# A transformer block in float32 on one core: part of the first MLP product by seven products of quarters in place of eight

## The chip, the core and the metric

The kernel runs on one core of a Trainium2 chip. The core has a matrix engine (TensorE, with its weight loads), VectorE, ScalarE, GpSimd (POOL in the profile) and SyncE (SP), which here issues nearly all transfers. [...] The metric is the device time of one execution in microseconds.

## The reference

One block: a layer norm without weights, attention, a second layer norm and an MLP, each with a residual. There are 2048 rows of 512, and 32 heads of 16.

```python
h = x + A(layernorm(x))
h2 = h + B(layernorm(h))

# A: qkv = x @ wqkv; each position attends to 8 positions at distances 0, 2, .. 14 behind it
logits = einsum("bhsd,bhswd->bhsw", q, kg) * Dh**-0.5      # masked where idx < 0
o = einsum("bhsw,bhswd->bhsd", softmax(logits), vg)
return o @ wo

# B: 512 -> 1792 -> 512, squared relu
h = x @ w1 + b1
r = where(h > 0, h, 0)
return (r * r) @ w2 + b2
```

## The kernel before

**Precision.** A float32 product is made of three passes in TensorE's faster float32 form: each operand is split into a high part (a cast by ScalarE) and the low rest (a subtraction by GpSimd or VectorE), and high x high, low x high and high x low are added in PSUM. `mm3` issues the three passes, each over four blocks of 128 in the contraction (`KB`).

**Tiles and stages.** The rows stand in 16 tiles of 128, in four groups `u` of four tiles (512 rows). First come qkv for all tiles. The attention of a group (`item`) is VectorE's and GpSimd's work and runs well ahead of its group's MLP. `to_mlp(u)` turns the attention's result, multiplies it with `wo` (`wo_product`), normalises, and turns the rows to the form the MLP wants; `split_h` then writes the high and low parts into the first four of twelve blocks of `big_h` and `big_l`.

**The MLP of a group.** The 1792 features are 14 blocks `f` of 128. For each, `mlp1(f)` multiplies w1's block with the group's 512 rows: 12 matmuls with 512 moving columns into one bank. ScalarE applies bias and relu, squares and casts, and the low part follows. `mlp2(f)` multiplies the result with w2's block: 12 matmuls into four banks (`acc`, one for each row tile), two blocks behind `mlp1` (`LAGW`). w1 is split once and stays: six blocks in `w1a_h`/`w1a_l`, eight in the other blocks of `big_h`/`big_l`. w2 is split once, written to DRAM, and read again for each block and group (`get_w2`, buffers `pair`). In the loop over `f` of group `u`, after block `TO_MLP`, stands `to_mlp(u + 1)`.

**The order.** Nothing of the order is written out by hand. Every operation is a task of `Plan`, with a duration for each engine that can do it, what it reads and writes, and the buffers that it takes (`bufs` has their numbers: six PSUM banks `ps`, one `qp`; the logits and exponentials `le` hold the eighth bank all the time). `deadlines` goes backwards from the TensorE tasks, whose places in time are the running sum `plan.pe`, and gives each task a due time with a random part (`NOISE`, one `SEED`). `schedule` is a list scheduler in simulated time: at each step the engine that can start first takes the ready task with the earliest due time. A transfer may start only `AHEAD` us before it is due; `KEEP` row buffers of a class are held back for more urgent tasks; `BEFORE` says how far ahead of its group the attention is due; `W2_EACH` spaces w2's splits; `X_BY_DRAM` lists the row tiles that are turned for qkv by DRAM and VectorE in place of TensorE. The instructions are then emitted in order of their simulated starts, and each engine and SP's queue run theirs strictly in that order. Semaphores come from the framework by what is read and written.

**What the profile's lines are.** L457 is the matmul in `mm`, of `mm3` (qkv, `wo`, first MLP product); L735 the matmul in `mlp2`; L955 the two half products at the very end; L401 a transpose by TensorE; L322 a cast (`hi`), L327 a low part (`lo`), L332 any sum through `tt`; L722, L724 relu and square; L572, L577, L603, L621 the attention.

Of the kernel before, what the change touches and what calls it, by code (L numbers as in the profile page):

```python
# [9 lines left out]
F32 = mybir.dt.float32  # L10
# [38 lines left out]
SEM = 0.15  # L49
AHEAD = 7.0  # L50
WAIT = {"DVE": 1.2, "ACT": 0.6, "POOL": 1.6, "SP": 0.8}
KEEP = 5
BUSY = 1.1
# [24 lines left out]
class Plan:  # L78
# [50 lines left out]
    def deadlines(self):  # L129

        draw = random.Random(SEED)
        for t in reversed(self.tasks):
            d = min([s.alap for s in t.succs], default=1e6) - t.dur - t.lat - WAIT.get(t.only, 1.0)
            t.alap = t.pe if t.pe is not None else d if t.by is None else min(d, t.by)
            t.due = t.alap + draw.uniform(-NOISE, NOISE)

    def schedule(self):
# [6 lines left out]
        for t in self.tasks:  # L144
            for b in t.bufs:
# [4 lines left out]
        queue = {tag: sorted((t for t in self.tasks if any(b.tag == tag for b in t.new)),  # L150
                             key=lambda t: t.due) for tag in (*ROWS, "pair")}
        while ready:
# [29 lines left out]
            if not best:  # L182
                held = {}
                for t in order:
                    for b in t.bufs:
                        if users[b]:
                            held.setdefault(b.tag, {})[b] = t
                raise RuntimeError([(o.n, round(o.start), round(o.due)) for o in order
                                    if o.on == "PE"][::40], [(t.n, [b.tag for b in t.new]) for t in ready][:12],
                                   {k: [(t.n, users[b]) for b, t in v.items()]  # L190
                                    for k, v in held.items()})
# [53 lines left out]
def block_kernel(ctx, tc, x, wqkv, wo, w1, b1, w2, b2, out):  # L245
# [23 lines left out]
    def where(t):  # L269
# [19 lines left out]
    w1a = (w1a_h, w1a_l)  # L289
    le = psum.tile([P, 2, R * W * GH], F32, name="le")  # L290

    bufs = {**ROWS, "pair": 4, "unit": 1, "kv": 3, "q": 1, "pr": 3, "o": 2, "ps": 6, "qp": 1,
            "st": 2, "mv": 4, "rs": 4, "sv": 6, "mx": 2, "sm": 2}
    pools = dict.fromkeys(("st", "mv", "rs", "sv", "mx", "sm"), small)
    pools.update(ps=psum, qp=psum, unit=wpool, pair=wpool)
    plan = Plan(bufs)
# [11 lines left out]
    def act(n, fn, extra=0.0, **k):  # L308
        return plan.add({"ACT": ac(n) + extra}, lambda e: fn(), **k)
# [232 lines left out]


    def window(t, i0, *ap):
        return bass.AP(tensor=t.tensor, offset=t.offset + i0 * GC,
                       ap=[list(t.ap[0]), [GC, IQ], [GC, W], *ap])

    def item(u, g, due, o):
# [17 lines left out]
        win(2, vs)  # L566
        lg = lambda: le[:, 0].rearrange("p (i w h) -> p i w h", i=R, w=W)
        ex = lambda: le[:, 1].rearrange("p (i w h) -> p i w h", i=R, w=W)
        lgs = [("lg", 0), ("lg", IQ)]
        for n, i0 in enumerate((0, IQ)):  # L570
            pr = buf("pr", (P, IQ, W, GC), name="pr")
            vec(2048, lambda pr=pr, i0=i0: nc.vector.tensor_tensor(  # L572
                out=pr.get(),
                in0=qp.get()[:, i0:i0 + IQ].unsqueeze(2).to_broadcast([P, IQ, W, GC]),
                in1=window(ks.get(), i0, [1, GC]), op=ALU.mult),
                r=[qp, ks], w=[pr], by=due + 5 * n)
            vec(2048, lambda pr=pr, i0=i0: nc.vector.tensor_reduce(  # L577
                out=lg()[:, i0:i0 + IQ].rearrange("p i w h -> p (i w h)"),
                in_=pr.get().rearrange("p i w (h d) -> p (i w h) d", d=DH), axis=X, op=ALU.add),
                r=[pr], w=[("lg", i0)], by=due + 5 * n + 1)  # L580
        if u < 2:
# [7 lines left out]
           ALU.subtract, r=[mx], w=lgs, by=due + 6)  # L589
        act(256, lambda: nc.scalar.activation(le[:, 1], le[:, 0], AF.Exp, scale=DH ** -0.5),  # L590
            r=lgs, w=["ex"], by=due + 6)
        vec(300, lambda: nc.vector.tensor_reduce(
            out=sm.get(), in_=ex().rearrange("p i w h -> p i h w"), axis=X, op=ALU.add),
            r=["ex"], w=[sm], by=due + 8)
        vec(64, lambda: nc.vector.reciprocal(sm.get(), sm.get()), w=[sm], by=due + 8)
        tt("DVE", 256, ex, ex, lambda: sm.get().unsqueeze(2).to_broadcast([P, R, W, GH]),
           ALU.mult, r=[sm], w=["ex"], by=due + 8)
        own = o is None
        if own:
            o = buf("o", (P, R, GC), name="o")  # L600
        for i0 in (0, IQ):
# [3 lines left out]
                in0=ex()[:, i0:i0 + IQ].unsqueeze(4).to_broadcast([P, IQ, W, GH, DH])),  # L605
                r=["ex", vs], w=[p2], by=due + 9 + i0)
            w = W // 2
# [50 lines left out]

    to_split = []

# [4 lines left out]
    def wo_product(t, oh, ol, h, pe, **k):  # L665
        ps = buf("ps", (P, D), name="wo")
        mm3(ps, ps.get, D, oh, ol, (lambda k: wo_h[:, k, :], [("wo", 0, k) for k in range(KB)]),
# [14 lines left out]
        def parts():  # L682
            if pe:
                view, src = lambda p: hh(p)[:, :, i, :], ht.get
            else:
# [3 lines left out]
               w=keys[1], engs=("DVE",) if pe else ("POOL", "DVE"))  # L689
        to_split.append(parts)  # L690


# [35 lines left out]

    def mlp2(f, hid, w2s, acc, js, first, last, split_):
        rh, rl = hid  # L730

        def run(terms, r, lead, end):
            def go(e):
                for n, (l, wn, j) in enumerate(terms):
                    nc.tensor.matmul(acc[j].get(), l.get()[:, j * P:(j + 1) * P],  # L735
                                     w2s.get()[:, wn], start=lead and n < len(js),
                                     stop=end and n >= len(terms) - len(js))
            plan.add({"PE": len(terms) * 0.23}, go, r=r, w=[acc[j] for j in js])
# [170 lines left out]
    split_h()  # L909
    w2s = {}  # L910
    for u in range(NU):
# [4 lines left out]
        engs = ("POOL", "DVE") if last else LO  # L916
        for f in range(FB):
            if u == 0 and f + FA < FB:
                w1_job(FA + f)
            w2s[f] = get_w2(f)  # L920
            hid[f] = mlp1(f, ("DVE",) if last and f >= FB - LAGW else engs)
            if f >= 2:
                g = f - 2
                if last and g == FB - 1 - LAGW:
                    mlp2(g, hid[g], w2s[g], acc, range(R - 1), g == 0, False, True)
                    mlp2(g, hid[g], w2s[g], acc, [R - 1], g == 0, True, False)
                else:
                    mlp2(g, hid[g], w2s[g], acc, range(R), g == 0, False, True)
            if not last and f == TO_MLP:
                to_mlp(u + 1, need[u + 1])  # L930
# [66 lines left out]
```

## Time and profile before

| | us |
|---|---|
| median of 3 runs | 515.17 (514.84 to 515.93) |
| the profiled execution | 514.67 |
| its span from first to last instruction | 512.9 |
| TensorE busy in it | 501.9 (98%) |
| VectorE, ScalarE, GpSimd busy | 333.6, 292.0, 323.0 |
| TensorE's clock, share of full | 1.00 |

The span is what the trace covers; 1.8 us of the profiled execution lie outside it. A matmul's busy time is its whole latency, and matmuls overlap, so the interval from start to start is what one costs in a row of them. A row of a group gives the line, engine, operation, tiles and shapes, the count, the busy time, the mean of one in ns, then the engine's idle time before them and what ended it.

### The profile page before, as it was taken

The numbers are of one execution on the slowest core, as the hardware profiler recorded it, in microseconds if no ns is written. First come the engines' busy times: TensorE is split into PE (matmuls) and PEld (weight loads), VectorE is DVE, ScalarE is ACT, GpSimd is POOL, SyncE is SP. The second block draws the span as 40 slices with busy tenths as digits, with TensorE's granted clock in tenths as the row PEclk, the third lists the DMA queues.
The fourth block names the chain that finished last, engine by engine and source line by source line (L and its number), as shares of the span: only waits on it lengthen the run. The fifth ranks groups of instructions, "written<-read, shape, count | busy, mean of one in ns | idle before, by whom it ended". The sixth has DMA issues, their size and how long they took to land.

```text
span 512.9 us, 6775 instructions
## 1 busy us (share of the span) xinstructions
PE 501.9 (98%) x2300; PEld 419.2 (82%) x2300; DVE 333.6 (65%) x314; ACT 292.0 (57%) x552; POOL 323.0 (63%) x273
## 2 busy tenths in 40 slices
PE   8999999999998999999999999999999999999997
PEld 8998888888886888868888877888888887888885
DVE  6259898996979996988799979596022103446003
ACT  4538877759364654379843436974367645433341
POOL 6421659768697799899994789589755424223220
PEclk9999999999999999999999999999999999999999
DMA  7699698999979999768976486865462731999422
GB/s 243 179 277 297 148 301 274 348 356 402 335 290 334 326 363 353 224 224 300 324 258 220 168 289 237 272 217 184 129 203 86 251 116 41 305 358 408 160 81 82
DMA packets 82834, 127.73 MB, mean 249 GB/s; under 512 B 7280, under 2 KB 49776, under 8 KB 82800
## 3 DMA queue, kind: packets, MB, share of 16 engines
q1 hardware_dynamic: 82656, 127.17, 73.3%
q8 instruction: 18, 0.29, 0.2%
q14 instruction: 16, 0.13, 0.1%
q10 hardware_dynamic: 144, 0.13, 0.1%
HBM read 89.96 MB, written 37.36 MB: 248 GB/s over the span
## 4 chain that ended last, share of the span: by engine, by line
PE 72%; DMA 8%; ACT 6%; POOL 5%; DVE 4%; issue 3%; SPq 1%; POOLq 0%; ACTq 0%; DVEq 0%
PE mm L457 41%; PE acc L735 20%; PE wo L457 7%; POOL pr L621 3%; DMA k<-qkv_d 3%; DVE pr L572 2%; PE tr L401 2%; DMA back<-o_d 2%; PE tr L803 1%; DMA qkv_d<-y 1%; DMA xt<-in_A_x_dram 1%; DMA o_d<-o 1%; POOL rl L327 1%; ACT r L722 1%; ACT big_h L322 1%
## 5 line engine op out<-in xcount | busy, mean ns | idle before, releaser
L621 POOL TENSOR_TENSOR pr<-pr 128x1024 f32<-128x1024 f32 (+1 forms) x64 | 118.8, 1883 | 11.7 <-DVE pr L603 8.4
L327 POOL TENSOR_TENSOR rl<-r,rh 128x512 fp32r<-128x512 f32 x53 | 68.6, 1297 | 86.4 <-ACT rh L322 86.2
L735 PE MATMUL acc<-w2s,rh 128*128 128x512 f32 x444 | 110.7, 389 | 0.0
L722 ACT ACTIVATE r<-mm,b_sb 128x512 f32<-128x512 f32 x56 | 38.3, 687 | 120.8 <-PE mm L457 113.8
L735 PEld LDWEIGHTS acc<-w2s,rh 128*128 128x128 f32 x444 | 83.3, 188 | 17.3
L572 DVE TENSOR_TENSOR pr<-qp,k 128x2048 f32<-128x2048 f32 x32 | 72.7, 2275 | 18.2 <-POOL o L621 12.7
L577 DVE TENSOR_REDUCE le<-pr 128x128 f32<-128x2048 f32 x32 | 73.3, 2290 | 0.9
L603 DVE TENSOR_TENSOR pr<-le,v 128x2048 f32<-128x2048 f32 x32 | 72.1, 2279 | 1.7 <-POOL o L621 1.1
L735 PE MATMUL acc<-w2s,rl 128*128 128x512 f32 x222 | 60.4, 390 | 0.0
L457 PE MATMUL mm<-big_h,xl 128*128 128x512 f32 (+1 forms) x208 | 51.1, 376 | 0.0
L457 PE MATMUL mm<-big_h,xh 128*128 128x512 f32 (+1 forms) x208 | 50.5, 375 | 0.1
L457 PE MATMUL mm<-big_l,xh 128*128 128x512 f32 (+1 forms) x208 | 50.6, 375 | 0.0
L735 PEld LDWEIGHTS acc<-w2s,rl 128*128 128x128 f32 x222 | 41.7, 188 | 9.0 <-DVE rl L327 0.4
L457 PEld LDWEIGHTS mm<-big_h,xh 128*128 128x128 f32 x208 | 38.0, 188 | 6.6 <-ACT big_h L322 0.5
L457 PEld LDWEIGHTS mm<-big_l,xh 128*128 128x128 f32 x208 | 37.9, 188 | 5.3
L457 PEld LDWEIGHTS mm<-big_h,xl 128*128 128x128 f32 x208 | 37.8, 188 | 5.2
L428 DVE STREAM_TRANSPOSE turned<-back 128x512 f32<-128x512 f32 x26 | 17.8, 696 | 36.6 <-DMA back<-o_d 24.1
L322 ACT CAST rh<-r 128x512 fp32r<-128x512 f32 x56 | 34.6, 622 | 3.0 <-ACT r L724 0.4
L724 ACT ACTIVATE r<-r 128x512 f32<-128x512 f32 x56 | 35.2, 632 | 1.3
L457 PE MATMUL mm<-big_h 128*128 128x512 f32 x128 | 34.5, 391 | 0.3 <-ACT r L722 0.3
L457 PE MATMUL mm<-big_h,big_l 128*128 128x512 f32 x128 | 34.2, 389 | 0.0
L457 PE MATMUL mm<-big_l,big_h 128*128 128x512 f32 x128 | 34.2, 389 | 0.0
(104 smaller groups left out, 791.2 us busy)
## 6 DMA issues: line engine op xcount, KB each, us to landing
w2s<-w_d SPq DMA_DIRECT2D x56, 512.0 KB, 5.0
k<-qkv_d SPq DMA_DIRECT2D x16, 704.0 KB, 6.1
v<-qkv_d SPq DMA_DIRECT2D x16, 704.0 KB, 6.2
qkv_d<-y SPq DMA_DIRECT2D x18, 512.0 KB, 3.6
raw<-in_B_w_dram SPq DMA_DIRECT2D x28, 256.0 KB, 6.7
w_d<-w2s SPq DMA_DIRECT2D x14, 512.0 KB, 6.6
xt<-in_A_x_dram SPq DMA_DIRECT2D x16, 256.0 KB, 5.7
q<-qkv_d SPq DMA_DIRECT2D x16, 256.0 KB, 4.3
```

The source lines that it names most:

```text
L322: act(n, lambda: nc.scalar.copy(dst(), src()), r=r, w=w, **k)
L327: lambda e: engines[e].tensor_tensor(out=dst(), in0=src(), in1=h(), op=ALU.subtract), r=r, w=w, **k)
L401: nc.tensor.transpose(tr.get()[:, n, :], s(), ident)
L428: vec(D, lambda: nc.vector.transpose(dst.get(), src.get()[:, part]), r=[src], w=[dst, *w])
L457: nc.tensor.matmul(ps(), l(), rr(), start=start and i == 0, stop=stop and i == len(terms) - 1)
L572: vec(2048, lambda pr=pr, i0=i0: nc.vector.tensor_tensor(out=pr.get(), in0=qp.get()[:, i0:i0 + IQ].unsqueeze(2).to_broadcast([P, IQ, W, GC ...
L577: vec(2048, lambda pr=pr, i0=i0: nc.vector.tensor_reduce(out=lg()[:, i0:i0 + IQ].rearrange("p i w h -> p (i w h)"), in_=pr.get().rearrange ...
L603: vec(2048, lambda p2=p2, i0=i0: nc.vector.tensor_tensor(out=p2.get(), in1=window(vs.get(), i0, [DH, GH], [1, DH]), op=ALU.mult, in0=ex()[ ...
L621: nc.gpsimd.tensor_tensor(out=dst, in0=a, in1=b_, op=ALU.add)
L722: act(D, lambda: nc.scalar.activation(r.get(), ps.get(), AF.Relu, bias=b1_sb[:, f:f + 1]), 0.08, r=[ps, "b1"], w=[r], keep=2)
L724: act(D, lambda: nc.scalar.activation(r.get(), r.get(), AF.Square), w=[r])
L735: nc.tensor.matmul(acc[j].get(), l.get()[:, j * P:(j + 1) * P], w2s.get()[:, wn], start=lead and n < len(js), stop=end and n >= len(terms) ...
```

## The change

For the third group of rows from the fourth pair of feature blocks on, and for the last group throughout, the first MLP product is made for two blocks at once. The 256 features x 512 (contraction) by 512 (contraction) x 512 (rows) are cut into halves in all three directions, and the four quarters of the result come from seven products of quarters and sums of them, in Winograd's form of Strassen's scheme, instead of eight products.

- `win_rows` makes the four sums of row quarters for two row tiles (`a`, `c`), from the turned rows, and splits them into high and low parts in blocks 4 to 7 of `big_h`/`big_l`, where parts of w1 lay.
- `win_weights` loads the pair's two blocks of w1 from DRAM again (two transfers of 256 KB), makes their four sums on GpSimd or VectorE, and splits all seven operands (casts of 512 and 768 columns, and as many low parts), in turn into blocks 8 to 11 of `big_h`/`big_l` and into `w1a_h`/`w1a_l`.
- `win_pair` makes the products: each is 6 matmuls with 256 moving columns (three passes over two contraction blocks) into half a bank. Three banks serve seven products: `X_` takes four of them (halves 0, 1, and again 0, 1), `Y` two, `Z`, which is the bank `qp` of the attention, one. ScalarE copies the first product out, and VectorE adds the others in, in seven additions of 256 columns. The relu then reads SBUF and not PSUM.
- In the loop over `f`, a pair takes two steps; second products follow for all blocks up to two behind.
- The `le` bank becomes a buffer of the plan, so that the last group's products with `wo` use it once the attention is over, in place of `ps`.
- Constants of the order: the random part has fourteen seeds, one for each 40 us of due time; `BEFORE` has 12 in place of 4 for the second group, `W2_EACH` 5 in place of 6, `AHEAD` 8 in place of 7, `KEEP` 3 in place of 5, `TO_MLP` 9 in place of 10; row tile 14 is turned by TensorE (`X_BY_DRAM`).

```diff
-BEFORE = 8, 4, 12, 8
-X_BY_DRAM = (14, 15)
-W2_EACH = 6.0
+BEFORE = 8, 12, 12, 8
+X_BY_DRAM = (15,)
+W2_EACH = 5.0
...
-NOISE, SEED = 0.3, 448
+NOISE, SEEDS = 0.3, (
+    842, 212, 503, 407, 141, 504, 671, 955, 219, 946, 769, 64, 289, 829)
+WIN = {2: (3, 4, 5, 6), 3: (0, 1, 2, 3, 4, 5, 6)}
...
-TO_MLP = 10
+TO_MLP = 9
...
-AHEAD = 7.0
+AHEAD = 8.0
...
-KEEP = 5
+KEEP = 3
...
-        draw = random.Random(SEED)
+        draws = [random.Random(n) for n in SEEDS]
...
+            draw = draws[max(0, min(int(t.alap // 40), len(draws) - 1))]
...
-    le = psum.tile([P, 2, R * W * GH], F32, name="le")
...
+    LE = buf("le", (P, 2, R * W * GH), name="le")
...
-        ps = buf("ps", (P, D), name="wo")
+        ps = buf("le" if t // R > min(WIN) else "ps", (P, D), name="wo")
...
+        if t // R in WIN:
+            hts[i] = ht
+            if i >= RI:
+                to_split.append(lambda: win_rows(hts[i - RI], hts[i], i - RI))
...
+    def win_rows(a, c, i):
+        t = buf("pair", (P, 4, 2 * P), name="t")
...
+            add_any(256, lambda n=n: tv(n), x, y, ALU.subtract, r=r, w=[(t, n)])
...
+        hi(1024, lambda: sums(0), src, r=ts, w=keys[0])
+        lo(1024, lambda: sums(1), src, lambda: sums(0), r=ts + keys[0], w=keys[1])
...
+    def win_weights(p, at_):
+        t = buf("pr", (P, 8, 2 * P), name="ws")
...
+        for j in range(2):
+            load(512, 512, lambda q, j=j: q.dma_start(
+                t.get()[:, 2 * j:2 * j + 2].rearrange("p n (k c) -> p (n k) c", k=2),
+                w1_v[2 * p + j]), w=[(t, 2 * j), (t, 2 * j + 1)], ahead=2 * AHEAD)
+        for n, x, y, op in ((4, 2, 3, ALU.add), (5, 4, 0, ALU.subtract), (6, 0, 2, ALU.subtract),
+                            (7, 1, 5, ALU.subtract)):
+            add_any(256, at(n), at(x), at(y), op, r=[(t, x), (t, y)], w=[(t, n)])
...
+    def win_pair(p, n, after):
+        banks = buf("ps", (P, 2, 2 * P), name="mm"), buf("ps", (P, 2, 2 * P), name="mm"), buf(
+            "qp", (P, 2, 2 * P), name="mm")
+        X_, Y, Z = banks
...
+        def product(bank, half, a, j, start, stop):
+            def go(e):
+                out_ = bank.get()[:, half]
+                terms = [(0, 0), (1, 0), (0, 1)]
+                for m, (pa, pb) in enumerate(terms):
+                    for kk in range(2):
+                        nc.tensor.matmul(out_, win_w(pa, n)[:, a, kk], win_b(pb, j, kk),
+                                         start=start and m + kk == 0,
+                                         stop=stop and m + kk == len(terms))
...
+        product(X_, 0, 0, 0, True, True)
+        act(256, lambda: nc.scalar.copy(h(m1, 0)(), h(X_, 0)()), r=[(X_, 0)], w=[(m1, 0)])
+        product(X_, 1, 4, 4, True, True)
+        dve(h(u, 0), h(X_, 1), h(m1, 0), ALU.add, [(X_, 1), (m1, 0)], [(u, 0)])
+        product(Y, 0, 5, 5, True, True)
+        dve(h(u, 1), h(Y, 0), h(u, 0), ALU.add, [(u, 0), (Y, 0)], [(u, 1)])
+        product(Y, 1, 3, 3, True, True)
+        dve(h(r1, 1), h(Y, 1), h(u, 1), ALU.add, [(u, 1), (Y, 1)], [(r1, 1)])
+        dve(h(r0, 1), h(Y, 1), h(u, 0), ALU.add, [(u, 0), (Y, 1)], [(r0, 1)])
+        product(Z, 0, 2, 6, True, True)
+        dve(h(r1, 0), h(u, 1), h(Z, 0), ALU.subtract, [(u, 1), (Z, 0)], [(r1, 0)])
+        product(X_, 0, 1, 1, True, True)
+        dve(h(r0, 0), h(X_, 0), h(m1, 0), ALU.add, [(X_, 0), (m1, 0)], [(r0, 0)])
+        product(X_, 1, 6, 2, True, True)
+        dve(h(r0, 1), h(X_, 1), h(r0, 1), ALU.add, [(X_, 1)], [(r0, 1)])
...
+            if f in pairs:
+                win_weights(f // 2, wins)
+                hid[f], hid[f + 1] = win_pair(f // 2, wins, [("second", u)] if f > 2 else [])
+                wins += 1
+            else:
+                hid[f] = mlp1(f, ("DVE",) if last and f >= FB - LAGW else engs)
+            f = fs[-1] + 1
+            for g in range(done, f - LAGW):
```

More of the change, by code (lines that the diff above doesn't have):

```diff
@@ L150, in schedule @@
         queue = {tag: sorted((t for t in self.tasks if any(b.tag == tag for b in t.new)),
-                             key=lambda t: t.due) for tag in (*ROWS, "pair")}
+                             key=lambda t: t.due) for tag in (*ROWS, "pair", "pr")}
         while ready:
@@ L187, in schedule @@
                             held.setdefault(b.tag, {})[b] = t
-                raise RuntimeError([(o.n, round(o.start), round(o.due)) for o in order
-                                    if o.on == "PE"][::40], [(t.n, [b.tag for b in t.new]) for t in ready][:12],
+                raise RuntimeError([(t.n, t.fn.__code__.co_firstlineno, round(t.due), [b.tag for b in t.new]) for t in ready],
                                    {k: [(t.n, users[b]) for b, t in v.items()]
@@ L727, in mlp1, with sums @@
         return rh, rl
-    def mlp2(f, hid, w2s, acc, js, first, last, split_):
+    def win_rows(a, c, i):
+        t = buf("pair", (P, 4, 2 * P), name="t")
+        top, low = slice(0, 2), slice(2, 4)
+        tv = lambda n: t.get()[:, n].rearrange("p (k r b) -> p k b r", k=2, b=KB)
+        for n, x, y, r in (
+                (0, lambda: by_row(c)[:, top], lambda: by_row(a)[:, top], [a, c]),
+                (1, lambda: by_row(c)[:, low], lambda: tv(0), [c, (t, 0)]),
+                (2, lambda: by_row(c)[:, low], lambda: by_row(c)[:, top], [c]),
+                (3, lambda: tv(1), lambda: by_row(a)[:, low], [a, (t, 1)])):
+            add_any(256, lambda n=n: tv(n), x, y, ALU.subtract, r=r, w=[(t, n)])
+        def sums(part):
+            return big[part][:, KB:2 * KB, :].rearrange("p j (k s m) -> p (j k) s m", k=2, s=2)[
+                :, :, i]
+        keys = [B(part, range(KB, 2 * KB), (i, 2 + i)) for part in range(2)]
+        src = lambda: t.get().rearrange("p n (k m) -> p (n k) m", k=2)
+        ts = [(t, n) for n in range(4)]
+        hi(1024, lambda: sums(0), src, r=ts, w=keys[0])
+        lo(1024, lambda: sums(1), src, lambda: sums(0), r=ts + keys[0], w=keys[1])
@@ new lines, in win_b, with win_b_keys, win_w @@
+    def win_b(part, n, kk):
+        if n < 3:
+            return big[part][:, (kk, 2 + kk, 2 + kk)[n], 2 * P * (n == 2):2 * P * (1 + (n == 2))]
+        return big[part][:, n + 1, 2 * P * kk:2 * P * (kk + 1)]
+    def win_b_keys(part, n):
+        if n < 3:
+            return B(part, ((0, 1), (2, 3), (2, 3))[n], (2, 3) if n == 2 else (0, 1))
+        return B(part, [n + 1], range(G))
+    def win_w(part, n):
+        t = (w1a[part].rearrange("p f k c -> p (f k c)") if n % 2 else
+             big[part][:, 2 * KB:, :].rearrange("p j n -> p (j n)"))
+        return t[:, :7 * 2 * P].rearrange("p (n k c) -> p n k c", n=7, k=2)
@@ new lines, in win_keys @@
+    def win_keys(part, n):
+        return ([("w1", part, f) for f in range(4)] if n % 2 else
+                B(part, range(2 * KB, 3 * KB), range(G)))
+    def win_weights(p, at_):
+        t = buf("pr", (P, 8, 2 * P), name="ws")
+        at = lambda n, m=1: lambda: t.get()[:, n:n + m]
+        for j in range(2):
[5 more added lines that the diff above has]
+            add_any(256, at(n), at(x), at(y), op, r=[(t, x), (t, y)], w=[(t, n)])
+        keys = [win_keys(part, at_) for part in range(2)]
+        for a, m, d in ((0, 2, 0), (3, 5, 2)):
+            r = [(t, n) for n in range(a, a + m)] + (keys[0] + keys[1]) * (d > 0)
+            view = lambda part, d=d, m=m: win_w(part, at_)[:, d:d + m].rearrange(
+                "p n k c -> p n (k c)")
+            ks = [[(*k, d) for k in kk] for kk in keys]
+            hi(256 * m, lambda view=view: view(0), at(a, m), r=r, w=ks[0] + keys[0] * (d == 0))
+            lo(256 * m, lambda view=view: view(1), at(a, m), lambda view=view: view(0),
+               r=r + ks[0], w=ks[1] + keys[1] * (d == 0), engs=("POOL", "DVE"))
@@ L730, in mlp2 @@
+    def mlp2(f, hid, w2s, acc, js, first, last, split_, more=[]):
         rh, rl = hid
@@ L737, in go @@
                                      stop=end and n >= len(terms) - len(js))
[L738 removed]
+            plan.add({"PE": len(terms) * 0.23}, go, r=r, w=[acc[j] for j in js] + more)
         one = [(rh, 0, j) for j in js] + [(rh, 1, j) for j in js]
@@ L909, in block_kernel @@
     split_h()
-    w2s = {}
+    w2s, wins = {}, 0
     for u in range(NU):
@@ L916, in block_kernel @@
         engs = ("POOL", "DVE") if last else LO
-        for f in range(FB):
+        pairs = {2 * p: p for p in WIN.get(u, ())}
+        f = done = 0
+        while f < FB:
+            fs = (f, f + 1) if f in pairs else (f,)
             if u == 0 and f + FA < FB:
                 w1_job(FA + f)
[L920 to L923, printed above, removed]
+            for g in fs:
+                w2s[g] = get_w2(g)
+            if f in pairs:
[6 more added lines that the diff above has]
+            for g in range(done, f - LAGW):
                 if last and g == FB - 1 - LAGW:
@@ L927, in block_kernel @@
                 else:
-                    mlp2(g, hid[g], w2s[g], acc, range(R), g == 0, False, True)
-            if not last and f == TO_MLP:
+                    mlp2(g, hid[g], w2s[g], acc, range(R), g == 0, False, True,
+                         [("second", u)] if g == 0 else [])
+                done = g + 1
+            if not last and TO_MLP in fs:
                 to_mlp(u + 1, need[u + 1])
```

55 lines of the change are left out of this document (43 added, 12 removed).

## The prediction

> **What bounds the kernel now.** I read the busy line and the slices of the page first.
>
> ```profile
> PE 501.9 (98%) x2300; PEld 419.2 (82%) x2300; DVE 333.6 (65%) x314; ACT 292.0 (57%) x552; POOL 323.0 (63%) x273
> ...
> PE   8999999999998999999999999999999999999997
> ...
> DVE  6259898996979996988799979596022103446003
> ...
> POOL 6421659768697799899994789589755424223220
> PEclk9999999999999999999999999999999999999999
> ```
>
> TensorE is busy 98% of the span at full clock in every slice. VectorE and GpSimd are close to full up to some 345 us and then mostly free. So TensorE's work sets the time, provided that it seldom waits. The view of waits says how seldom:
>
> ```profile
> engine line waited for: us in total, times, longest us
> PE mm L457 <- DVE big_l L327: 2.0, 1, 2.0
> PE wo L457 <- ACT oh L322: 1.9, 2, 1.2
> PE tr L803 <- POOL ident masks.py:199: 1.3, 1, 1.3
> PE mm L457 <- ACT big_h L322: 0.9, 1, 0.9
> PE tr L401 <- ACT y L534: 0.4, 1, 0.4
> PE mm L457 <- ACT r L722: 0.3, 1, 0.3
> PE wo L457 <- ACT r L722: 0.2, 1, 0.2
> ```
>
> That is 7.0 us in the whole span. Busy time counts a matmul's whole latency, so for a price I want the interval between starts. The timeline of TensorE in the third group of tiles has the steady loop of the two MLP products (rows of the first product's first pass, one feature block apart):
>
> ```profile
> 409.59 1.07 PE L457 MATMUL mm<-big_h 128*128 128x512 f32 x4
> ...
> 415.03 1.07 PE L457 MATMUL mm<-big_h 128*128 128x512 f32 x4
> ...
> 420.47 1.07 PE L457 MATMUL mm<-big_h 128*128 128x512 f32 x4
> ```
>
> A block is 12 matmuls of the first product and 12 of the second, and takes 5.44 us: 0.2267 us for a matmul with 512 moving columns. For the narrow one the chain of waits has 12 matmuls with 256 columns at the very end, each with its own weights and six adding into one place, as the new products do; and groups of transposes with 128 columns:
>
> ```profile
> 108.41 0.96 PE tr L401 x8
> ...
> 507.71 1.44 PE half L955 x12
> ```
>
> That is 1.44/12 = 0.120 us for 256 columns and 0.96/8 = 0.120 us for a transpose. Half the columns cost 53% of the interval, not 50%.
>
> **The change, term by term.** *Removed and put in on TensorE.* A pair of feature blocks costs 24 x 0.2267 = 5.44 us in the first product now. With seven products of two k blocks, three passes each, it is 42 matmuls of 256 columns: 42 x 0.120 = 5.04 us. 0.40 us a pair; four pairs in the third group of tiles and seven in the last give 11 x 0.40 = 4.40 us. One row tile (14) goes from the DMA transpose back to TensorE: 4 x 0.120 = 0.48 us. TensorE's own sum is 3.92 us less.
>
> [...]
>
> *Put on the other engines, per pair.* The rows are these, of the groups kept apart by shape:
>
> ```profile
> L590 ACT ACTIVATE le<-le 128x256 f32<-128x256 f32 x16 | 6.1, 383 | 5.5 <-DVE le L332 5.5
> L322 ACT CAST w2s<-raw 128x512 fp32r<-128x512 f32 x14 | 8.6, 623 | 0.4 <-DMA raw<-in_B_w_dram 0.4
> L332 DVE TENSOR_TENSOR le<-le,mx 128x256 f32<-128x256 f32 x16 | 6.8, 424 | 0.2
> L621 POOL TENSOR_TENSOR o<-pr 128x256 f32<-128x256 f32 x32 | 23.8, 754 | 0.1
> L327 POOL TENSOR_TENSOR rl<-r,rh 128x512 fp32r<-128x512 f32 x53 | 68.6, 1297 | 86.4 <-ACT rh L322 86.2
> ```
>
> VectorE combines the products in seven additions of 256: 7 x 0.424 = 3.0 us. ScalarE copies one product (0.38) and casts weights of 512 and 768 columns (0.62, and by its width about 0.93): 1.9 us. The weights' four sums and two low parts cost GpSimd at most 4 x 0.754 + 2.5 x 1.297 = 6.3 us, or less than half of that where VectorE takes them. The room is in the last two of these stretches:
>
> ```profile
> 59.00:125.00 66.00, 66.00 (x311) 55.26 (x310) 58.27 (x53) 49.59 (x117) 52.66 (x45) 1.00 0.95 319
> ...
> 345.00:408.00 63.00, 63.00 (x277) 51.52 (x277) 16.61 (x20) 36.55 (x68) 42.96 (x34) 1.00 0.54 177
> 430.00:500.00 70.00, 70.00 (x310) 57.97 (x309) 21.46 (x27) 25.75 (x41) 16.59 (x13) 1.00 0.67 240
> ```
>
> (Columns: length, then busy TensorE, weight load, VectorE, ScalarE, GpSimd, clock, DMA share, GB/s.) Four pairs in the stretch from 345 us bring VectorE to 28.6 of 63 us, ScalarE to 44 and GpSimd to at most 68, of which VectorE can take a part. The last stretch has more room. So this is hidden, at nothing; without that cover it would be up to 6.3 us for a pair. A pair's results are wanted only after the following pair and the second products of the pair before it, some 10 us later, so the longer way through ScalarE and GpSimd is covered too.
>
> *DMA.* Two loads of 256 KB of the first weights come back for each pair, 22 issues on SP's queue. They land like the earlier loads of these weights, and are asked for 16 us ahead:
>
> ```profile
> raw<-in_B_w_dram SPq DMA_DIRECT2D x28, 256.0 KB, 6.7
> ```
>
> 512 KB in a pair's 10.5 us is some 50 GB/s on a stretch that moves 177 to 240 GB/s while 319 GB/s were reached over the first of the three rows above. Hidden; queued behind a load that waits for its buffer would be the second weights, which have four buffers. I take 0.
>
> *New waits inside a pair.* The seven products use three PSUM banks, two halves in each. The sixth product writes again into the half that the first used, and the copy of the first and the sum of the second must have left that bank. With 0.72 us per product it starts 3.6 us after the first. The second product ends at 1.44 us, plus 0.16 of pipeline (282 ns of latency, first row below, against 120 of interval); the copy then takes 0.38 and the sum 0.42: done at 2.4, so 1.2 us of slack. An instruction ahead on the same queue could eat it; the longest there are the other two rows:
>
> ```profile
> L955 PE MATMUL half<-w2s,rh 128*128 128x256 f32 x8 | 1.6, 282 | 0.0
> ...
> L390 ACT ACTIVATE hn<-h,sv 128x512 f32<-128x512 f32 x12 | 15.7, 1309 | 0.4
> L332 DVE TENSOR_TENSOR m<-m,b 128x512 f32<-128x512 f32 x12 | 11.6, 967 | 7.7 <-DMA m<-m_d 7.7
> ```
>
> Both at once would hold TensorE for 1.1 us (1.309 + 0.967 - 1.2). Bounds: 0, and three pairs hit by that, 3.3 us. I take 0.3 us in all, near the lower end, as both engines idle over half of the last stretch.
>
> *The step into the last group of tiles.* The timeline of ScalarE there, and the row of TensorE's that followed it:
>
> ```profile
> 420.67 0.69 ACT L722 ACTIVATE r<-mm,b_sb 128x512 f32<-128x512 f32 x1 [3.38 <-PE mm L457]
> 421.40 0.63 ACT L724 ACTIVATE r<-r 128x512 f32<-128x512 f32 x1
> 422.12 0.62 ACT L322 CAST rh<-r 128x512 fp32r<-128x512 f32 x1
> 424.30 2.95 ACT L322 CAST big_h<-turned 128x512 fp32r<-128x512 f32 x3 [1.56 <-PE mm L457]
> ...
> 427.61 1.10 ACT L322 CAST big_h<-turned 128x512 fp32r<-128x512 f32 x1
> ```
>
> ```profile
> 428.76 1.19 PE L457 MATMUL mm<-big_h,w1a_h 128*128 128x512 f32 x4 [0.87 <-ACT big_h L322]
> ```
>
> Now the four casts of the next activations must wait for the last first product, with 2 x 2.72 us of second products as main cover, and 0.87 us shows. After the change four second products lie between, 10.9 us, and 1.4 us more for the sums, whose last reader is the fifth product. In it ScalarE has the casts (2.95 + 1.10 = 4.1), two casts of the sums (1024 columns each, between 0.62 and 2 x 1.1; say 1.25) and the last pair's six passes (twice 0.69, 0.63 and 0.62): 4.1 + 2.5 + 3.9 = 10.5 us, then a low part. It fits with about 1 us over, or misses by as much. Bounds: 0.9 us gained, 3 us lost (GpSimd taking the low parts last). I take no change.
>
> *Order and constants.* Seeds, the lead of the second group's attention, transfers taken 8 us ahead instead of 7, W2's spacing, one row class's reserve: these reorder the queues from the start to the end. The trace can't price that. From below, all waits but the start's 1.3 us gone: 5.7 us gained. From above, the waits of 7.0 us up by half: 3.5 us lost. I take 0.
>
> **The sum.** The profiled execution took 514.67 us (its span 512.9 and 1.8 around it), 0.50 under the median of the runs, 515.17. 514.67 - 4.40 + 0.48 + 0.3 = 511.05; on the median, 511.55. Forecast: 511.5 us.
>
> **Rivals.** *The order also heals waits.* Where half of the 5.7 us goes: 511.5 - 2.9 = 508.6. For it: they are single waits at transitions, not a steady loss. Against: VectorE and GpSimd stay full up to 345 us, and nothing is taken from them there.
>
> *The cover fails at the transitions, no change.* 3 us at the last step and another 0.8 inside the pairs give 511.5 + 3.0 + 0.8 - 0.3 = 515.0. For it: the ScalarE sum fills its cover nearly whole. Against: the first, sixth and seventh products need no sums.
>
> *TensorE waits for the reader of the shared bank: slower.* If the second product may not start before the copy out of the other half of its bank has ended, each pair has a wait of 0.16 + 0.38 + some 0.05 for the signal = 0.59 us, more than the 0.40 saved: 515.17 + 0.48 + 11 x 0.19 = 517.7. It decides from 0.36 us a pair (3.92/11). For it: two halves of a bank are in use by two engines in turn throughout. Against: if the second product stands ahead of the copy in program order, as it does where TensorE is free at once, the copy waits and not the matmul.
>
> [...]
>
> *Narrow matmuls don't hold their interval: slower.* 0.120 us rests on 12 in a row. Were the weight load's latency the interval, a pair would cost 42 x 0.191 = 8.0 us and the time be 515.17 + 0.48 + 11 x 2.58 = 544:
>
> ```profile
> L955 PEld LDWEIGHTS half<-w2s,rh 128*128 128x128 f32 x8 | 1.3, 191 | 0.0
> ```
>
> Against: these 12 had just such loads and ran at 0.120; so did the transposes.
>
> **Chances.** Forecast 0.63, healed waits 0.14, cover fails 0.13, bank waits 0.08, interval 0.02. A measurement of this kernel tells about 0.2%, 1.03 us, from no change, so faster is below 514.1. The forecast and the healed waits count for faster, and a fifth of the failed cover: 0.80. Same 0.10, slower 0.10. The likeliest case's own range, waits by their nearer bounds, is 509.5 to 513.5; the range reaches to the healed case and to the failed cover: 508.4 to 514.9.
>
> **What would show it.** Right: some 200 more matmuls on TensorE; the seven products of a pair, 42 matmuls, in 5.0 us; in the last group's loop a period of 10.48 us a pair (5.04 + 5.44) where it was 10.88; waits of TensorE within 2 us of 7.0 in sum. Wrong: TensorE idle between the products of a pair for ScalarE's copy or VectorE's sums, over 0.36 us in most pairs; an idle time of several us ahead of the last group's first pair; waits for weights of a pair; or new waits before 345 us from the new order, where nothing else changes but the one tile.

## The result and the profile after

The changed kernel takes 536.03 us (median of 6 runs, 535.0 to 536.63) where the kernel before took 514.85 us beside it (6 runs): 1.0412 times as long, with a 95% interval of 1.0389 to 1.0435. The forecast was 511.5 us. It is slower by 21 us, far outside the range of 508.4 to 514.9.

The busy line and the slices of the changed kernel:

```profile
PE 508.5 (95%) x2502; PEld 431.1 (81%) x2502; DVE 435.1 (81%) x445; ACT 314.5 (59%) x590; POOL 379.8 (71%) x303
...
PE   8999999999998999999999999997999988889897
...
DVE  6279989998969899499898799898394998969843
...
PEclk9999999999998999999999999999999997979999
```

TensorE has its 202 more matmuls. VectorE, which was to be busy 33 us more for the seven additions, and something for the weights, is busy 101.5 us more, and its last twelve slices, at 0.0 to 0.6 before, stand at 0.3 to 0.9, seven of them at 0.8 or more. TensorE's clock, full throughout before, has slices at 0.7. The waits of TensorE are 22.2 us in sum where they were 7.0 (engine, line waited for, us in total, times, longest):

```profile
PE mm L823 <- DVE u L333: 5.3, 3, 3.6
PE mm L823 <- DVE big_l L328: 4.5, 1, 4.5
PE acc L871 <- ACT rh L323: 2.8, 1, 2.8
PE mm L458 <- DVE big_l L328: 2.4, 1, 2.4
PE acc L871 <- POOL rl L328: 1.6, 1, 1.6
```

Line 823 is the matmul of the seven products, 871 that of the second product, 333 and 328 are the sums and low parts, 804 the sums in SBUF that the change adds. The mean clock over the span is the other loss:

```profile
core 0: 534.5 us, clock 0.980
```

The span grew from 512.9 to 534.5 us, by 21.6. TensorE's own sum gives -3.9 and its waits 22.2 - 7.0 = 15.2. The clock withheld 0.020 x 534.5 = 10.7 us, some of it while TensorE waited anyway. What it cost is read from the matmuls behind the waits of 2.40, 2.79, 4.49 and 3.60 us: up to the next group at full clock they take 1.6, 1.8, 2.5 and 2.8 us more than 0.2267 or 0.120 us each, 8.7 us in sum. Together that is 20.0 us; 1.6 us are not placed. The first of these waits also stands in the run with all constants and no pairs (below), so it does not come from the pairs. Nor is the clock a fixed share: the mean clocks of the six runs reach from 0.980 to 0.994, and their times differ by 1.6 us only.

The products themselves are as fast as forecast. The timeline of TensorE has one pair's seven products in a row; each line is one pass of two matmuls, and the last row is what follows:

```profile
451.84 0.40 PE L823 MATMUL mm<-big_h,w1a_h 128*128 128x256 f32 x2
...
456.64 0.40 PE L823 MATMUL mm<-big_l,w1a_h 128*128 128x256 f32 x2
456.88 2.00 PE L871 MATMUL acc<-w2s,rh 128*128 128x512 f32 x8
```

42 matmuls in 456.88 - 451.84 = 5.04 us. The largest wait shows where the time goes instead. First TensorE at the step into the last group:

```profile
428.53 2.00 PE L871 MATMUL acc<-w2s,rh 128*128 128x512 f32 x8
...
438.50 0.40 PE L823 MATMUL mm<-big_h,big_l 128*128 128x256 f32 x2
443.39 0.76 PE L823 MATMUL mm<-big_l,big_h 128*128 128x256 f32 x2 [4.49 <-DVE big_l L328]
...
445.23 3.49 PE L871 MATMUL acc<-w2s,rh 128*128 128x512 f32 x8
```

It waits 4.49 us for a low part of the row sums. After it eight matmuls of the second product take 3.49 us, which took 2.00 before it, at a granted clock of 0.52 from 445.20 to 448.60 us. VectorE and GpSimd in the same stretch:

```profile
438.20 2.58 DVE L804 TENSOR_TENSOR ws<-ws 128x256 f32<-128x256 f32 x1 [0.64 <-POOL ws L804]
440.70 2.54 DVE L328 TENSOR_TENSOR big_l<-t,big_h 128x1024 fp32r<-128x1024 f32 x1
```

```profile
438.13 2.36 POOL L328 TENSOR_TENSOR big_l<-t,big_h 128x1024 fp32r<-128x1024 f32 x1
440.45 4.19 POOL L328 TENSOR_TENSOR big_l<-turned,big_h 128x512 fp32r<-128x512 f32 x2
```

A sum of 256 columns takes VectorE 2.58 us. It begins when GpSimd's low part has begun, and ends just after it; then VectorE's own low part, which takes 1.21 us in the mean in the run below whose order knows of the exclusion, takes 2.54: it waits for the first of GpSimd's next two (440.45 to 442.17 us). The two pass each other by turns. The groups of VectorE kept apart by shape show which sums suffer (mean of one in ns behind the busy time):

```profile
L804 DVE TENSOR_TENSOR ws<-ws 128x256 f32<-128x256 f32 x27 | 27.9, 1040 | 0.7 <-POOL ws L804 0.6
L333 DVE TENSOR_TENSOR m<-m,b 128x512 f32<-128x512 f32 x12 | 15.1, 1261 | 0.0
L333 DVE TENSOR_TENSOR m<-m,h 128x512 f32<-128x512 f32 x12 | 14.2, 1190 | 0.0
...
L333 DVE TENSOR_TENSOR u<-mm,m 128x256 f32<-128x256 f32 x11 | 4.6, 419 | 17.2 <-PE mm L823 13.4 <-ACT r L852 2.0 <-ACT m L836 1.4
```

`u<-mm,m` has one operand in PSUM (`mm`, what TensorE wrote) and takes 419 ns; `ws<-ws` has the same shape with both operands in SBUF and takes 1040. The last sums of the parked rows, which the change does not touch, go from 967 and 691 ns to 1261 and 1190.

### The profile page after: what moved, and what is told of

Read it like the earlier page. It is cut to its first block, busy times and chain, and to the rows that moved or that the text cites. A ratio compares the mean times of both kernels' runs of the same rounds, so it can differ in the third digit from the quotient of the medians.

```text
span 534.5 us, 7447 instructions
## 1 busy us (share of the span) xinstructions
PE 508.5 (95%) x2502; PEld 431.1 (81%) x2502; DVE 435.1 (81%) x445; ACT 314.5 (59%) x590; POOL 379.8 (71%) x303
## 4 chain that ended last, share of the span: by engine, by line
PE 45%; DVE 14%; ACT 5%; POOL 4%; issue 3%; DMA 1%; SPq 0%; DVEq 0%; POOLq 0%; ACTq 0%
PE acc L871 19%; PE mm L458 13%; PE mm L823 7%; PE wo L458 6%; DVE m L333 3%; DVE t L804 2%; DVE big_l L328 2%; ACT big_h L323 2%; DVE pr L576 2%; DVE ws L804 1%; POOL pr L626 1%; DVE r L333 1%; POOL t L804 1%; ACT hn L391 1%; DVE pr L608 1%
## 5 line engine op out<-in xcount | busy, mean ns | idle before, releaser
L626 POOL TENSOR_TENSOR pr<-pr 128x1024 f32<-128x1024 f32 (+1 forms) x64 | 120.4, 1897 | 10.3 <-DVE pr L608 7.3
L871 PE MATMUL acc<-w2s,rh 128*128 128x512 f32 x444 | 115.4, 400 | 2.8 <-ACT rh L323 2.8
L328 POOL TENSOR_TENSOR rl<-r,rh 128x512 fp32r<-128x512 f32 x47 | 65.8, 1403 | 54.3 <-ACT rh L323 48.3
L731 ACT ACTIVATE r<-mm,b_sb 128x512 f32<-128x512 f32 x34 | 23.3, 686 | 47.6 <-PE mm L458 47.5
L458 PE MATMUL mm<-big_l,xh 128*128 128x512 f32 (+1 forms) x208 | 49.4, 375 | 0.0
L328 POOL TENSOR_TENSOR big_l<-ws,big_h 128x512 fp32r<-128x512 f32 (+1 forms) x9 | 19.1, 2126 | 14.8 <-ACT big_h L323 13.2
L535 ACT COPY y<-mm 128x512 f32<-128x512 f32 x36 | 20.8, 586 | 14.8 <-PE mm L458 13.0
L804 DVE TENSOR_TENSOR ws<-ws 128x256 f32<-128x256 f32 x27 | 27.9, 1040 | 0.7 <-POOL ws L804 0.6
L852 ACT ACTIVATE r<-r,b_sb 128x512 f32<-128x512 f32 x22 | 15.4, 721 | 20.6 <-DVE r L333 20.6
L328 POOL TENSOR_TENSOR w2s<-raw,w2s 128x512 fp32r<-128x512 f32 x14 | 18.1, 1297 | 9.0 <-ACT w2s L323 9.0
```

The costliest lines, as they stand in the source:

```text
L328: lambda e: engines[e].tensor_tensor(out=dst(), in0=src(), in1=h(), op=ALU.subtract), r=r, w=w, **k)
L458: nc.tensor.matmul(ps(), l(), rr(), start=start and i == 0, stop=stop and i == len(terms) - 1)
L626: nc.gpsimd.tensor_tensor(out=dst, in0=a, in1=b_, op=ALU.add)
L731: act(D, lambda: nc.scalar.activation(r.get(), ps.get(), AF.Relu, bias=b1_sb[:, f:f + 1]), 0.08, r=[ps, "b1"], w=[r], keep=2)
L804: lambda e: engines[e].tensor_tensor(out=out_(), in0=a(), in1=b(), op=op), **k)
```

## The experiments

Theory P, formed from these rows: VectorE's sums of two SBUF operands and GpSimd's sums shut each other out; the order was made without that, so VectorE's queue runs late and TensorE waits for it, and after a long wait its clock is about half for a while (0.52 granted above). Rivals: O, the new constants and seeds make a worse order by themselves; S, something in each pair (copies, sums, halves of banks) holds TensorE by a fixed amount; G, GpSimd's queue is simply too long.

### Same order, GpSimd writes constants in the pairs' code

```diff
+    def fill(dst, n):
+        for _ in range(2):
+            nc.gpsimd.memset(dst.bitcast(F32), 0.5)
...
-                 lambda e: engines[e].tensor_tensor(out=out_(), in0=a(), in1=b(), op=op), **k)
+                 lambda e: fill(out_(), n) if e == "POOL" else engines[e].tensor_tensor(
+                     out=out_(), in0=a(), in1=b(), op=op), **k)
```

(and so for the low parts in `win_rows`, `win_weights` and `win_pair`)

> The changed kernel with its order untouched; where the pairs' code has GpSimd make a sum or a low part (22 of the sums, the weights' and the sums' low parts, the results' low parts), GpSimd writes a constant twice instead, which takes some 85% as long and reads nothing. Those operands are left out of the computation. Theory P (VectorE's sums of two SBUF operands and GpSimd's sums shut each other out, so VectorE's queue runs late and TensorE waits for it): VectorE's sums of 256 in the pairs go from a mean of 1.04 us to about 0.41, its busy time from 435 to under 400 us, the waits of TensorE from 22 us to 10 or less, the time to 510 to 516 us. Rival O (the new constants and seeds make a worse order by themselves): 530 to 537 us, as the order is the same. Rival S (the chain of copies and sums inside a pair, or the halves of banks, hold TensorE): 530 to 537 us, the waits for VectorE's sums of the products unchanged.

Measured: 519.0 us, 1.0083 times the kernel before (1.0052 to 1.0115). Of the 21 us, 17 go. Groups of VectorE, and the starts of the second products that follow each pair in TensorE's timeline (in this kernel line 808 is the sum in SBUF, 804 the constant write, 833 the seven products and 881 the second product):

```profile
L808 DVE TENSOR_TENSOR ws<-ws 128x256 f32<-128x256 f32 x27 | 18.1, 678 | 1.7 <-POOL ws L804 1.6
L333 DVE TENSOR_TENSOR m<-m,b 128x512 f32<-128x512 f32 x12 | 8.1, 684 | 1.5 <-DMA m<-m_d 1.5
L333 DVE TENSOR_TENSOR m<-m,h 128x512 f32<-128x512 f32 x12 | 8.1, 683 | 0.0
```

```profile
469.52 2.00 PE L881 MATMUL acc<-w2s,rh 128*128 128x512 f32 x8
...
480.05 2.00 PE L881 MATMUL acc<-w2s,rh 128*128 128x512 f32 x8
...
491.01 2.00 PE L881 MATMUL acc<-w2s,rh 128*128 128x512 f32 x8
...
501.53 2.00 PE L881 MATMUL acc<-w2s,rh 128*128 128x512 f32 x8
```

With nothing read by GpSimd there, the parked rows' sums take 684 ns again, and the last group runs at 10.53, 10.96 and 10.52 us a pair where 10.48 was forecast. Rivals O and S fall: order, products, banks and VectorE's additions are the same. The writes need no input either, so GpSimd no longer waits there for ScalarE's casts; how much of the 17 us that gives, this run does not show. The parked rows' sums, which the edit does not touch, show the exclusion apart from it. Measured 519.0 misses P's range of 510 to 516 by 3 us. TensorE's waits are still 11.7 us in sum, where 10 or less were expected: `ws<-ws` stays at 678 ns (946 from 330 to 380 us, where GpSimd still makes the attention's sums, and 528 from 420 us on), and waits at 361, 371, 394 and 440 us remain. VectorE's busy time came to 404.6 us and not under 400.

### The same with three writes

```diff
-        for _ in range(2):
+        for _ in range(3):
```

> As the run with two constant writes in place of each of GpSimd's sums and low parts in the pairs' code, with three writes, so that GpSimd is occupied about a fifth longer than by the sums themselves (3 x 0.316 = 0.95 us for 256 columns against 0.75, 3 x 1.17 = 3.5 us for 1280 against some 3.0). The same operands are left out of the computation. Theory P (the sums shut each other out): GpSimd's length hardly matters, 517 to 524 us. Rival G (GpSimd's queue is simply too long, and the two writes helped because they were 15% shorter): 533 us or more.

Measured: 523.33 us, 1.0190 (1.012 to 1.026). GpSimd is now busy 387.1 us, more than the 379.8 of the changed kernel, and 13 us of the 21 are still gone. G as the whole cause falls; GpSimd's length has a part, 4 us between two and three writes, where TensorE waits for its results (2.1 us for `big_l` of line 804, there the constant write).

### The disputed costs alone

A kernel that computes nothing of the block: groups of VectorE sums of 256 columns beside other work on GpSimd, then groups of 40 matmuls with growing idle times ahead.

```python
sums(12, a)               # both operands in SBUF
pool(6); sums(12, a)      # beside sums of 1280 on GpSimd
pool(6); sums(12, ps)     # one operand in PSUM, beside the same
fill(8); sums(24, a)      # both in SBUF, beside constant writes
```

> Computes nothing of the block; it measures the disputed costs alone. VectorE sums 128 x 256: with nothing on GpSimd; beside GpSimd sums of 1280; the same with one operand in PSUM beside GpSimd sums; beside constant writes by GpSimd. Then groups of 40 matmuls of 512 columns with idle times of TensorE that grow from about 0.6 to 5 us, twice. Theory P: 0.41 us alone; about 3 us, the length of the GpSimd sum, beside GpSimd sums (one VectorE sum for each); 0.42 with PSUM; 0.41 beside writes. Rival (the two share the memory's bandwidth): all three concurrent groups slower by like factors. Clock: after idle times of some 2.5 us and more the matmuls take 427 ns for some us, after shorter ones 227 ns throughout.

Measured, by groups of VectorE in stretches of the span: alone (10.2 to 14.9 us), beside GpSimd's sums (35.5 to 53), with one operand in PSUM (whole span), beside writes (79 to 88.7):

```profile
L85 DVE TENSOR_TENSOR c<-a,b 128x256 f32<-128x256 f32 x11 | 4.7, 425 | 0.4
...
L85 DVE TENSOR_TENSOR c<-a,b 128x256 f32<-128x256 f32 x6 | 18.2, 3038 | 0.2
...
L85 DVE TENSOR_TENSOR c<-ps,b 128x256 f32<-128x256 f32 x12 | 5.1, 424 | 0.4
...
L85 DVE TENSOR_TENSOR c<-a,b 128x256 f32<-128x256 f32 x22 | 9.4, 426 | 0.8
```

425 ns alone, 3038 ns beside GpSimd's sums of 3012 ns, one for one, and 424 and 426 ns in the other two. In these rows it is an exclusion of whole instructions, not a sharing of bandwidth, and it shows only where VectorE has two SBUF operands and GpSimd an instruction that reads: not with one operand in PSUM (424 ns), not beside writes (426 ns). What in the chip makes it, they do not show.

The clock, in TensorE's timeline (start, length of the group, idle ahead in brackets):

```profile
17.80 9.40 PE L121 MATMUL acc<-mv,st 128*128 128x512 f32 x40 [1.42 <-ACT mv L119]
29.26 10.96 PE L121 MATMUL acc<-mv,st 128*128 128x512 f32 x40 [2.06 <-ACT mv L119]
...
72.28 12.13 PE L121 MATMUL acc<-mv,st 128*128 128x512 f32 x40 [4.01 <-ACT mv L119]
89.08 10.68 PE L121 MATMUL acc<-mv,st 128*128 128x512 f32 x40 [4.66 <-ACT mv L119]
```

After 1.42 us of idle time 40 matmuls take 9.40 us; after 2.06 us they take 1.56 more, and after longer ones 1.3 to 2.7 more, on top of the wait. The granted clock was 1.00 in the first of these groups and 0.84 over the second. That is so in this run; the last section has waits of like length in the kernels that cost nothing on top.

### The parts of the change

All constants and seeds, no pairs (`WIN = {}`, and the products with `wo` in `ps` as before):

> The changed kernel without pairs (every first product as before), with all new constants, seeds and row tile 14 turned by TensorE. Theory P: 513 to 517 us, within 0.5% of the kernel before, as TensorE has 0.48 us more and the order is as tight as before. Rival O: 525 us or more, most of the 21 us lost.

Measured: 515.85 us, 1.0018 (1.0003 to 1.0033). Theory O falls: the order without pairs is as good as before, within 0.9 us, of which 0.48 are the added transposes' by their row.

Pairs in the third group only. In this kernel the last group's first product reads what the pairs left where w1 stood, so that group isn't the block's; its work and order are:

```diff
-WIN = {2: (3, 4, 5, 6), 3: (0, 1, 2, 3, 4, 5, 6)}
+WIN = {2: (3, 4, 5, 6)}
```

> Pairs only in the third group (4 of 11), constants and seeds as in the changed kernel. Theory P: the waits of the changed kernel at 361, 369 and 394 us and the slow clock after one of them stay, those from 420 us on go: 518 to 526 us. Rival O: as the changed kernel, 530 us or more. Rival S (a fixed loss for each pair, 21 us over 11 pairs): 515 + 4 x 1.9 = 522 us, so against S this run counts only with the next one.

Measured: 524.31 us, 1.0191 (1.0169 to 1.0213).

Pairs in the last group only (`WIN = {3: (0, 1, 2, 3, 4, 5, 6)}`):

> Pairs only in the last group (7 of 11), constants and seeds as in the changed kernel. Theory P: the waits at the step into the last group and beside the last sums of the parked rows stay, those from 345 to 400 us go: 522 to 532 us. Rival O: 530 us or more. Rival S: 515 + 7 x 1.9 = 528 us.

Measured: 531.24 us, 1.0309 (1.0275 to 1.0342). Both halves lose, 9 and 16 us, and 9 + 16 is more than the 21 of all. Per pair that is 2.3 and 2.3 us, a little over the 1.9 that S forecast; taken alone these two runs do not tell P from S, the constant writes do.

### An order that knows of the exclusion

```diff
+                    if eng == "POOL" or eng == "DVE" and t.port:
+                        s = max(s, lock)
...
+            if eng == "POOL" or eng == "DVE" and t.port:
+                lock = end
...
-        plan.add({"POOL": po(n), "DVE": dv(n) + 0.15},
+        plan.add({"DVE": dv(n)},
```

`t.port` marks sums of two SBUF operands; the pairs' sums and low parts go to VectorE alone. First with the seeds of the changed kernel:

> All eleven pairs and the same computation, but the scheduler is told that an operation on GpSimd and a sum of two SBUF operands on VectorE exclude each other, and the pairs' sums and low parts all go to VectorE. Constants and seeds as in the changed kernel. Theory P1 (the loss is only that the order was made in ignorance of it): 511 to 519 us. Theory P2 (with the exclusion there isn't time enough on VectorE and GpSimd for the pairs' work, whatever the order): 524 to 536 us, with VectorE over 90% busy beside the pairs.

Measured: 534.92 us, 1.0399 (1.0357 to 1.0442). Inconclusive. It came out within P2's range, but VectorE was not over 90% busy beside the pairs (72.9 of 90 us from 430 to 520), and two waits that have nothing to do with pairs, at 205 and 222 us, took 4.9 us, with the granted clock at 0.8 in the slice from 201 to 214 us: those seeds belong to another order. The exclusion is gone from the pairs here: GpSimd is busy 6.7 of these 90 us, and `ws<-ws` takes 425 ns. Still TensorE's waits are 22.0 us in sum, 10.9 of them past 380 us. So taking the exclusion out of the pairs does not by itself bring the time back; the order has to fit as well. The seeds were searched afresh:

> All eleven pairs and the same computation, scheduler told of the exclusion, the pairs' sums and low parts on VectorE, and now the seeds, AHEAD 8, KEEP 4, TO_MLP 8 and W2_EACH 5 searched afresh with a replay of the queues in which the two engines exclude each other (the run before this one kept seeds that were chosen without it, and had waits at 205 and 222 us that have nothing to do with pairs). Theory P1 (only the ignorance of the order costs): 511 to 516 us. Theory P2 (the pairs' work on VectorE also costs waits that no order found avoids): 518 to 526 us, the sum of TensorE's waits from 380 us on 5 us or more.

Measured: 518.17 us, 1.0068 (1.0038 to 1.0098). The largest waits of TensorE:

```profile
PE mm L829 <- DVE r L338: 2.2, 1, 2.2
PE wo L463 <- ACT oh L327: 1.7, 3, 0.8
PE mm L829 <- DVE big_l L332: 1.5, 1, 1.5
```

The same eleven pairs in an order that knows of the exclusion lose 3 us and not 21. It lies in P2's range, with 4.0 us of waits of the seven products themselves (2.2, 1.5 and 0.3) and 4.4 in all from 380 us on, where P2 expected 5 or more. It differs from the run before it by seeds and two constants (`KEEP`, `TO_MLP`), so the 17 us between the two are a matter of the order. That no order of all eleven pairs gains is not shown, only that this search found none.

### Only as many pairs as VectorE has room for

Pairs 3 to 6 of the last group, whose weights' sums go to VectorE and whose results' low parts to GpSimd; the first eight parked rows are summed up 40 us earlier, the last four 11 to 14; seeds searched in the same way, by a replay of the queues with the exclusion. `W2_EACH` and `TO_MLP` are as in the kernel before, `KEEP` is 4.

```diff
+WIN = {3: (3, 4, 5, 6)}
...
+                 r=[("md", t), ("turn", t % 3)] + ([("md", NT - R - 1)] if t >= 2 * R else []), w=[m],
+                 by=due, ahead=AHEAD + 4)
...
-        unpark(n, plan.pe - 76 + 5 * n)
+        unpark(n, plan.pe - 116 + 5 * n if n < 2 * R else plan.pe - 50 + 6 * (n - 2 * R))
```

> Only the last group's last four pairs (3 to 6), whose w1 blocks may be overwritten by then; the pairs' sums and weights' low parts on VectorE, the results' low parts on GpSimd; the last sums of the first eight parked rows drawn 40 us ahead into the stretch from some 390 us; seeds searched with the exclusion, BEFORE 8, 12, 12, 8, W2_EACH 6, row tile 14 by TensorE. TensorE's own sum: 4 x 0.40 less, 0.48 more, 1.1 us. Theory P: the pairs' work fits, TensorE waits for no sum of a pair for over 0.5 us, 511.5 to 514.5 us, some 1 us under the run without pairs of the same call. Rival S (each pair loses by itself): 516 us or more.

And without any pair, seeds searched as long (`KEEP` is 5):

> The same without any pair, with seeds searched in the same way and as long: what the search and the moved last sums do alone. 512.5 to 515 us.

Measured: with four pairs 511.78 us, 0.9946 (0.992 to 0.9972) of the kernel before; without pairs 512.31 us, 0.9968 (0.9945 to 0.999). Both are faster than the kernel before, by less than 1%, and the four pairs beat the changed kernel by 24 us. The intervals of the two runs overlap: 0.5 us between them is no measured gain of the pairs. What is shown is that four pairs do not lose. The run without pairs lies just under the 512.5 to 515 expected of it. TensorE waits for no product's sum in the profile of the four, taken of their longest execution (516.3 us); its longest waits are of the second product:

```profile
PE acc L871 <- ACT rh L322: 2.8, 2, 1.9
PE acc L871 <- POOL rl L327: 1.9, 1, 1.9
```

## Why the prediction was wrong, step by step

**TensorE's own sum: right.** 0.40 us a pair from 0.120 us for 256 columns: 42 matmuls took 5.04 us, and with the reading of GpSimd taken away the pairs' loop ran at 10.52 to 10.96 us for the 10.48 forecast.

**The other engines' load, "this is hidden, at nothing": the step that failed.** The price of VectorE's seven additions came from a row with one operand in PSUM (424 ns) and was right: they took 409 to 419 ns, 31.4 us in all. What failed is the rest. The weights' work was put at "less than half" of GpSimd's 6.3 us a pair where VectorE takes it, and the row sums' work on the two engines was not priced at all. But sums with both operands in SBUF cost 425 ns alone and up to the length of GpSimd's instruction, 3.0 us, beside it: `ws<-ws` took 1040 ns on VectorE, longer than the 754 ns of GpSimd's own row. By the rows kept apart by shape, VectorE spent 60.7 us on sums and low parts of weights and rows, 20.0 of them for the rows, and 9.5 us more on the parked rows' sums than before. The stretches of the changed kernel that answer to those of before:

```profile
345.00:408.00 63.00, 57.64 (x281) 47.52 (x280) 46.77 (x54) 36.37 (x63) 49.11 (x35) 0.97 0.49 162
430.00:500.00 70.00, 60.92 (x343) 53.09 (x341) 59.80 (x80) 35.29 (x55) 50.99 (x34) 0.90 0.73 239
```

From 345 to 408 us the forecast had VectorE busy 28.6 us; it was 46.8. The sign stood in the profile before: the prediction quoted the parked rows' first sum, 967 ns in the mean, and two groups of sums of the same shape stand beside it there,

```profile
L332 DVE TENSOR_TENSOR h<-wo,h 128x512 f32<-128x512 f32 x16 | 10.8, 684 | 16.7 <-PE wo L457 16.7
...
L332 DVE TENSOR_TENSOR m<-m,h 128x512 f32<-128x512 f32 x12 | 8.2, 691 | 4.3 <-DMA h<-h_d 4.0
```

with 684 and 691. The 967 was read as a long instruction, not as some that wait. The timelines of GpSimd and VectorE before show one that waits, out of a group whose median is 693 ns:

```profile
462.12 1.29 POOL L327 TENSOR_TENSOR rl<-r,rh 128x512 fp32r<-128x512 f32 x1 [4.26 <-ACT rh L322]
```

```profile
462.29 1.66 DVE L332 TENSOR_TENSOR m<-m,b 128x512 f32<-128x512 f32 x1 [0.52 <-DMA m<-m_d]
```

"Room" was counted for each engine by itself, when it had to be counted for both together.

A smaller error in the same term: the weights' second part has 1280 columns, not 768, which the list of the change has wrong too. Its cast took 1.27 us and GpSimd's low part about 3.0, so a pair's work on GpSimd was at most 4 x 0.754 + 1.3 + 3.0 = 7.3 us and not 6.3.

**Waits inside a pair: bounds too low.** 0.3 us with at most 3.3; measured 5.3 for `u`, 1.0 for ScalarE's copy and 0.9 for `r`, 7.2 us. The slack of 1.2 us covered a pair with an empty queue, such as the one from 451.84 us above; the largest wait, 3.6 us, came behind parked rows' sums that themselves waited for a low part of GpSimd:

```profile
463.71 3.38 POOL L328 TENSOR_TENSOR w1a_l<-ws,w1a_h 128x1280 fp32r<-128x1280 f32 x1
```

```profile
464.22 4.02 DVE L333 TENSOR_TENSOR m<-m,b 128x512 f32<-128x512 f32 x2
```

**The step into the last group: bounds too low.** No change forecast, at most 3 us lost; 4.5 us measured, for a low part of the row sums that stood behind a 256-column sum of 2.58 us and then waited itself. The count of ScalarE's casts, on which the bound rested, was not what ended last.

**The clock: missing from the sum.** No term was there for it, since the kernel before never showed it: its longest wait was 2.04 us, with the clock full after it. In the changed kernel about half the clock was granted for some us after the waits of 2.4 to 4.5 us (0.52 from 165.3 to 168.7 us, 0.50 from 374.3 to 376.0, 0.52 from 443.4 to 448.7, 0.51 from 469.8 to 475.9), and that cost 8.7 us, 7.1 of them after waits that the run without pairs does not have.

**Constants of the order: right.** 0 forecast; 515.85 us with all of them and no pairs. But they were chosen for an order without the exclusion, and how much an order's fit is worth the two runs of eleven pairs above show.

**Rivals.** Waits for the shared bank are out: the same products at the same banks ran at 5.04 us a pair, and TensorE waited 1.0 us in all for ScalarE's copy (0.72 and 0.29 us, the second product starting 0.05 us after the copy's end). Where the product stood ahead, the reader waited: VectorE's sum of the sixth product began at 457.08 us, after the seventh in the other half of the bank, which ended at 457.04, and not after the sixth, at 456.32. Narrow matmuls that lose their interval are out by the same 5.04 us. The cover that fails at the transition was the nearest, but its mechanism was ScalarE's casts, and its price stopped at 515.0. Healed waits played no part with these seeds; a fresh search of seeds, with the parked rows' sums moved, took 2.7 us off without any pair by the medians (515.04 - 512.31), and 0.1 to 0.55% by the interval.

## What to carry to other kernels

Before work is moved to engines that look idle, ask for each instruction where both operands lie: on VectorE a sum of two SBUF operands took as long as the reading GpSimd instruction beside it (3038 ns beside 3012, 425 alone), and one with an operand in PSUM took no longer there (424). A group whose mean is well above that of another of the same shape (967 against 684 ns) can be a wait inside the instruction, and an order made without it runs late: here by 21 us. After waits of 2.4 to 4.5 us TensorE was granted about half its clock for some us (0.50 to 0.52), which cost up to 2.8 us a wait here; after one of 2.72 us in another run it cost nothing.

## What the runs showed of the hardware beside this

GpSimd and VectorE pass by turns: in the run of the disputed costs six sums of each went one for one, so GpSimd, whose instructions are the longer ones, loses little and VectorE nearly everything. Six of GpSimd's took 18.46 us beside VectorE's two-operand sums and 17.95 alone, twelve of VectorE's 21.16 us and 5.47 with one operand in PSUM:

```profile
34.75 21.16 DVE L85 TENSOR_TENSOR c<-a,b 128x256 f32<-128x256 f32 x12
...
56.67 5.47 DVE L85 TENSOR_TENSOR c<-ps,b 128x256 f32<-128x256 f32 x12
```

```profile
16.11 17.95 POOL L89 TENSOR_TENSOR pc<-pa,pb 128x1280 f32<-128x1280 f32 x6 [6.22 <-DVE pa L97]
34.86 18.46 POOL L89 TENSOR_TENSOR pc<-pa,pb 128x1280 f32<-128x1280 f32 x6 [0.80 <-DVE pa L97]
```

The clock fell after less idle time than was supposed: in the run of the disputed costs 2.06 us were enough in both series, 1.41 and 1.42 us were not, and the loss of 1.3 to 2.7 us for 40 matmuls does not grow steadily with the idle time. In the kernels the length alone does not decide. With four pairs a wait of 1.91 us was followed by eight slow matmuls; with three writes they kept their interval after 2.72 us:

```profile
251.59 2.77 PE L871 MATMUL acc<-w2s,rh 128*128 128x512 f32 x8 [1.91 <-ACT rh L322]
```

```profile
373.50 2.12 PE L881 MATMUL acc<-w2s,rh 128*128 128x512 f32 x8 [2.72 <-ACT rh L323]
```

Undisturbed, eight such matmuls take 2.00 us. What else decides is not shown.
